# Converting float64 weights with three Vector steps, an intermediate word in PSUM, and banks lent for it

## The chip, the cores and the metric

The kernel runs on one core of a Trainium2 chip. The core has five engines that matter here, each with its own in-order queue: PE (matmuls, with PEld for the loading of its weights), DVE (the Vector engine), ACT (the Scalar engine), POOL (GpSimd) and SP, which issues the DMAs. PSUM, where matmuls write, has eight banks of 2 KiB per partition. The metric is the device time of one execution in microseconds.

## The reference

Inputs are q, k, v of shape 8 x 8 heads x 576 x 64 in float32, and the weights U (576 x 32), V (32 x 576), w_ch1 (512 x 2048) and w_ch2 (2048 x 512). The weights come in as float64.

```python
# attention: pooled by 4 over the sequence, plus local with |i - j| < 4
out_up = np.repeat(sm_attn(q_d, k_d, v_d), 4, axis=2)
scores = np.where(mask, scale * q @ k.T, -1e9)
x = (out_up + softmax(scores) @ v)         # to B, S, 512
# mixing over the sequence and a channel FFN
h = xt @ U @ V
u = x + h.transpose(0, 2, 1)
ch = np.maximum(u @ w_ch1, 0.0) @ w_ch2
return (u + ch).astype(np.float32)
```

## The kernel before

**Precision.** PE multiplies in a reduced float32 form, so u, the hidden layer and the weights are each kept as a high word (H) and a low word (L = value - H). Each product is three matmuls: H by H, H by L, L by H.

**The weights.** `convert` turns float64 words into a float32 value t, then into H and L. A float64 is read as two int32 words, w(1) the high one (sign, 11 bits of exponent, 20 of mantissa), w(0) the low one. For a block of 128 x 512: ACT takes the absolute value of the high word as a float (L341); DVE clamps it (L342), shifts it left by 5 and right by 2 (L344), puts the sign and the top exponent bit back (L347) and puts in the top three bits of the low word (L349); ACT writes H (L351); POOL writes L = t - H (L354). All four DVE steps read and write SBUF. W1 is 16 such blocks (`load_w1`), W2 16 (`load_w2`); U is converted in two layouts (`load_ublk`, early; `load_u`, late) and V in two halves (`load_v`). The raw words of W1, W2 and the late U share three buffers (tag "Pt", with the products of the late attention), taken in the order W1, W2, U.

**The work.** There are 32 pairs of heads (4 for each of 8 batch elements). The first five are "early": their local attention runs on PE (`local_blocks`: scores in `ps_b`, transposes in `ps_bt`, values in `ps_ba`), their pooled attention in `early_global`. The other 27 are "late": pooled attention on PE, the local part as products on POOL (L799) and sums on DVE (L804). `early_mix` and `mix_part` apply U and V and write uH and uL. The FFN then runs over 256 steps (8 batch elements x 2 halves of 288 columns x 16 blocks of the hidden layer). `ffn1` of a step is 12 matmuls into one bank `ps_h` (L888), then ACT writes hH (L895) and DVE hL (L896) from that bank; `ffn2` is 12 matmuls (L911) into four output banks acc0 to acc3, which are kept over 16 steps. `ffn2` of a step is planned three steps after its `ffn1` (LAG = 3) and just ahead of the `ffn1` that is then due. hH has four buffers, hL three.

**PSUM before.** Four banks of one tag each in `ps_acc` (acc0 to acc3): FFN-2's sums, and before them the early scores, alternating between acc0/acc1 and acc2/acc3. Two banks of one tag in `ps_h`: FFN-1, and before it the early transposes and values. Two banks in `ps_m` for everything else.

**What sets the order.** The program lists operations with an engine, an estimated duration, a priority and what they read and write. A planner (`Plan.run`) simulates the five engines with these estimates and writes out each engine's queue; a buffer is granted to the operation that heads its queue (by priority among kinds that share a slot), and freed when its last user is done. On the chip every engine works through its queue in that order. FFN matmuls have the lowest priority and fill what attention leaves. W2 lies in the SBUF of the early attention: "late" is the point at which all early operations are done, and the high words of W2 and FFN-1 steps from 3 on wait for it.

## Time and profile before

| what | value |
|---|---|
| runs of the kernel | 1036.84, 1036.84 and 1039.56 us (median 1036.84) |
| span of the profiled execution, the only time that the page gives of it | 1036.6 us |
| ACT writing H of W1, 16 blocks | 10.0 us, 628 ns each |
| ACT writing H of W2, 16 blocks | 10.0 us, 627 ns each |
| POOL writing L of W1, 16 blocks | 22.8 us, 1425 ns each |
| POOL writing L of W2, 16 blocks | 24.1 us, 1506 ns each |
| loads of W1 and of W2 | 16 DMAs of 512 KB each |

A line of a group names the source line, the engine, the operation, the tile written and the tiles read, the shapes, how often it ran; then the busy time in us and the mean of one in ns; then the idle time of its engine before it and what ended it. A line of windows gives, for a stretch of time, each engine's busy time with the number of its instructions, the granted clock of PE as a share of full speed, the busy share of the DMA engines and GB/s. The chain of waits follows the work that ended last back in time and gives each line's share of the stretch. A line of waits gives the time in total, the number and the longest. A line of the timeline gives the start, the duration, the engine and the operation. "c" is the converted block's tile t of W1 or W2; w1r and w2r are the raw words.

### The profile page before, as it was taken

Reading aid. Unit: us, or ns where it says so; the run is one execution under the profiler, and the core shown is the slowest. Engines: PE = TensorE matmul, PEld = TensorE weight load, DVE = VectorE, ACT = ScalarE, POOL = GpSimd, SP = SyncE. Lnnn points to the kernel's source line nnn. Section 1 sums busy time; section 2 is a strip of 40 time slices with the busy share of each in tenths; the row PEclk is TensorE's granted clock in tenths of the full one; section 3 lists DMA queues with packets and bytes.
Section 4 is the critical chain, followed back from the end, with each engine's and each line's share of the span. In section 5 each row is a group of like instructions: output and inputs, shape, how many; then the busy total and the mean of one; then the engine's idle time right before and its main releaser. Section 6 shows DMA issues by size and latency. Waiting matters only on the chain.

```text
span 1036.6 us, 26946 instructions
## 1 busy us (share of the span) xinstructions
PE 996.9 (96%) x10831; PEld 975.3 (94%) x10831; DVE 529.8 (51%) x1054; ACT 388.0 (37%) x1234; POOL 557.2 (54%) x567
## 2 busy tenths in 40 slices
PE   6778898999999999999999999999999999999998
PEld 5667888999999999999999999999999999999998
DVE  5997898655554545444475344534652544211111
ACT  3676554442443434443344244423443232111110
POOL 4854568788575656565585638762765625211010
PEclk9896999999999999999999999999999999999999
DMA  8866764753555545545555355624644242000000
GB/s 279 226 172 179 199 186 116 149 138 104 135 137 115 141 113 132 128 86 146 120 137 125 87 132 133 143 75 101 151 116 117 64 113 50 24 1 24 1 24 23
DMA packets 222612, 120.30 MB, mean 116 GB/s; under 512 B 175492, under 2 KB 198456, under 8 KB 222488
## 3 DMA queue, kind: packets, MB, share of 16 engines
q1 hardware_dynamic: 222488, 118.58, 45.5%
q8 instruction: 85, 1.39, 0.6%
q14 instruction: 39, 0.32, 0.1%
HBM read 87.78 MB, written 30.75 MB: 114 GB/s over the span
## 4 chain that ended last, share of the span: by engine, by line
PE 84%; DVE 7%; POOL 3%; issue 2%; DMA 2%; ACT 2%; SPq 0%; DVEq 0%; POOLq 0%; ACTq 0%
PE acc L911 36%; PE ps_h L888 35%; PE ps_a L552 2%; PE ps_b L719 2%; DVE c L347 2%; PE ps_hu L848 1%; DVE c L349 1%; PE ps_t L539 1%; DMA w2r<-in_W 1%; PE ps_b L726 1%; POOL Pt L799 1%; DVE c L342 1%; DVE c L344 1%; PE ps_a L484 1%; PE ps_v L431 1%
## 5 line engine op out<-in xcount | busy, mean ns | idle before, releaser
L911 PE MATMUL acc<-hH,W2H 128*128 128x288 f32 x1024 | 310.5, 303 | 0.0
L896 DVE SCALAR_TENSOR_TENSOR hL<-ps_h,hH 128x288 fp32r<-128x288 f32 x256 | 116.6, 455 | 378.6 <-ACT hH L895 378.0
L888 PE MATMUL ps_h<-uH,W1H 128*128 128x288 f32 x1024 | 304.3, 297 | 4.1 <-DVE hL L896 3.1
L911 PE MATMUL acc<-hH,W2L 128*128 128x288 f32 x1024 | 303.1, 296 | 2.6 <-POOL W2L L354 2.6
L888 PE MATMUL ps_h<-uL,W1H 128*128 128x288 f32 x1024 | 303.4, 296 | 1.2 <-POOL uL L871 1.2
L911 PE MATMUL acc<-hL,W2H 128*128 128x288 f32 x1024 | 302.6, 296 | 0.0
L888 PE MATMUL ps_h<-uH,W1L 128*128 128x288 f32 x1024 | 302.0, 295 | 0.0
L799 POOL TENSOR_TENSOR Pt<-vl,at 128x896 f32<-128x896 f32 (+1 forms) x135 | 233.4, 1809 | 115.1 <-DVE acc L804 61.1
L895 ACT ACTIVATE hH<-ps_h 128x288 fp32r<-128x288 f32 x256 | 105.1, 410 | 433.6 <-PE ps_h L888 433.5
L888 PEld LDWEIGHTS ps_h<-uH,W1H 128*128 128x128 f32 x1024 | 193.5, 189 | 5.4 <-DVE hL L896 3.8
L911 PEld LDWEIGHTS acc<-hH,W2L 128*128 128x128 f32 x1024 | 193.2, 189 | 3.5 <-POOL W2L L354 3.5
L888 PEld LDWEIGHTS ps_h<-uL,W1H 128*128 128x128 f32 x1024 | 193.4, 189 | 1.5 <-POOL uL L871 1.5
L911 PEld LDWEIGHTS acc<-hH,W2H 128*128 128x128 f32 x1024 | 193.3, 189 | 1.1
L888 PEld LDWEIGHTS ps_h<-uH,W1L 128*128 128x128 f32 x1024 | 193.7, 189 | 0.0
L911 PEld LDWEIGHTS acc<-hL,W2H 128*128 128x128 f32 x1024 | 193.7, 189 | 0.0
L804 DVE TENSOR_REDUCE acc<-Pt 128x128 f32<-128x1024 f32 (+1 forms) x135 | 144.7, 1103 | 4.7 <-POOL Pt L799 2.3
L871 POOL TENSOR_TENSOR uL<-xT,uH 128x288 fp32r<-128x288 f32 x56 | 44.1, 811 | 71.3 <-ACT uH L869 71.2
L921 POOL TENSOR_TENSOR o<-uH,uL 128x288 f32<-128x288 f32 x64 | 49.8, 816 | 54.2 <-DMA out_t<-o 54.2
L840 POOL TENSOR_TENSOR xL<-xL,xH 116x640 fp32r<-116x640 f32 x28 | 44.0, 1572 | 64.2 <-ACT xH L839 49.3
L510 POOL TENSOR_TENSOR vr<-vr 72x256 f32<-72x256 f32 x54 | 42.4, 785 | 46.9 <-DMA vr<-in_v 46.8
L793 ACT ACTIVATE Pt<-ul 128x128 f32<-128x128 f32 (+1 forms) x135 | 48.4, 441 | 21.3 <-DVE acc L804 20.0
L744 ACT ACTIVATE se<-ps_b 96x114 f32<-96x114 f32 x108 | 38.5, 357 | 47.1 <-PE ps_b L719 34.1
(129 smaller groups left out, 1106.9 us busy)
## 6 DMA issues: line engine op xcount, KB each, us to landing
vl<-in_vp SPq DMA_DIRECT2D x54, 240.0 KB
out_t<-o SPq DMA_DIRECT2D x64, 144.0 KB
w1r<-in_W SPq DMA_DIRECT2D x16, 512.0 KB
w2r<-in_W SPq DMA_DIRECT2D x16, 512.0 KB
Y<-x_s SPq DMA_DIRECT2D x112, 72.0 KB
gT<-in_kT SPq DMA_DIRECT2D x27, 291.0 KB
xL<-x_s SPq DMA_DIRECT2D x28, 280.0 KB
gq<-in_qT SPq DMA_DIRECT2D x27, 288.0 KB
```

What stands on the lines that cost most here:

```text
L510: pool_tt(256, lambda x=x: nc.gpsimd.tensor_tensor(out=x()[:, :, 0:2, :], in0=x()[:, :, 0:2, :], in1=x()[:, :, 2:4, :], op=ALU.add), [x], ...
L744: act(n * KL, lambda p=ps[hh], se=se, n=n, rows=rows: nc.scalar.activation(se()[rows, 0:n].rearrange("p r k -> p (r k)"), p()[rows, 0:n * ...
L793: act(n * D, lambda n=n, ps=ps, Pt=Pt: nc.scalar.activation(Pt()[:, :n, :, 7], ul()[:, ps, :], AF.Copy), [ul], [(Pt, 1)], prio, 0.16)
L799: nc.gpsimd.tensor_tensor(out=Pt()[:, :n, :, 0:7].rearrange("p s d o -> p o s d"), in0=win, in1=at()[:, ps, :].rearrange("p s o -> p o s") ...
L804: dve(8.5 * n * D, lambda n=n, ps=ps, Pt=Pt: nc.vector.tensor_reduce(out=acc()[:, ps, :], in_=Pt()[:, :n], axis=AX.X, op=ALU.add), [(Pt, 0 ...
L840: pool_tt(640, lambda: nc.gpsimd.tensor_tensor(out=xL(), in0=xL().bitcast(F32), in1=xH().bitcast(F32), op=ALU.subtract), [xL, xH], [xL], prio)
L871: pool_tt(TN, lambda uH=uH, uL=uL, uf=uf: nc.gpsimd.tensor_tensor(out=uL()[:, hp, :], in0=uf(), in1=uH()[:, hp, :].bitcast(F32), op=ALU.su ...
L888: nc.tensor.matmul(ps()[:, :TN], w[:, dc, fs], u()[:, dc, :], start=(n == 0), stop=(n == 3 * NDC - 1))
L895: last_h[i] = act(TN, lambda: nc.scalar.activation(hH(), ps()[:, :TN], AF.Relu), [ps], [hH], FIRST, 0.05)
L896: dve(TN, lambda: nc.vector.scalar_tensor_tensor(hL(), ps()[:, :TN], 0.0, hH().bitcast(F32), op0=ALU.max, op1=ALU.subtract), [ps, hH], [hL ...
L911: nc.tensor.matmul(ac[e]()[:, :TN], W2[w][:, fc, es], hx(), start=(fc == 0 and n == 0), stop=(fc == NFC - 1 and n == 2))
L921: pool_tt(TN, lambda e=e, o1=o1: nc.gpsimd.tensor_tensor(out=o1()[:, :TN], in0=uH()[:, e, :].bitcast(F32), in1=uL()[:, e, :].bitcast(F32), ...
```

## The change

`convert` loses the clamp. ACT now copies the high word with a scale of 2^-112, which moves the exponent's bias; DVE shifts that left by 3 into a tile y in PSUM, puts the sign from w(1) into y, and then writes t from y and w(0). y lies in the second FFN-1 bank (h1) for W2 and for the late U, and else in acc2 and acc3 by turns. The early scores use acc0 and acc1 alone. The two `ps_h` banks have a tag each: FFN-1 steps 0 to 18 use h0 only, later ones h0 and h1 by turns, and from step 19 on each FFN-1 also depends on the one before it in the plan. The first FFN-2 step waits for the high words of all W1 blocks. The estimated durations of the conversion's DVE steps are new as well.

```diff
@@ -16,8 +16,6 @@
 AF = mybir.ActivationFunctionType
 ALU = mybir.AluOpType
 AX = mybir.AxisListType
-F_MIN = float(np.uint32(0x38000000).view(np.float32))
-F_MAX = float(np.uint32(0x47EFE000).view(np.float32))
 
 PE, DVE, ACT, POOL, SP = range(5)
 SLACK_FROM = 80
@@ -223,6 +221,7 @@
     PWx = 0.5
     pw = lambda prio: PW0 if prio < 10 else PWx
     W1P = 20
+    H1 = NFC + LAG
     NE = 5
     CN = 512
     QL, KL = 32, 38
@@ -243,7 +242,7 @@
     ffn = ctx.enter_context(tc.tile_pool(name="ffn", bufs=1))
     dram = ctx.enter_context(tc.tile_pool(name="dram", bufs=1, space=bass.MemoryType.DRAM))
     ps_acc = ctx.enter_context(tc.tile_pool(name="ps_acc", bufs=1, space=bass.MemoryType.PSUM))
-    ps_h = ctx.enter_context(tc.tile_pool(name="ps_h", bufs=2, space=bass.MemoryType.PSUM))
+    ps_h = ctx.enter_context(tc.tile_pool(name="ps_h", bufs=1, space=bass.MemoryType.PSUM))
     ps_m = ctx.enter_context(tc.tile_pool(name="ps_m", bufs=2, space=bass.MemoryType.PSUM))
 
     def psum(pool, name, tag, bufs):
@@ -295,6 +294,7 @@
     pat_sb = early_pool.tile([128, KW - KL], F32, name="pat_sb")
     Ublk = early_pool.tile([128, NS, 2 * R], F32, name="Ublk")
     kept = {}
+    count = {"y": 0}
 
     def ring(shape, name, n=2):
         if name not in kept:
@@ -334,20 +334,23 @@
 
     def convert(raw, pp, n, hi_out, lo_out, a, wkey, name, prio, gate=(), l0=0):
         t = buf(ffn, [128, CN], I32, name, "cT:" + name, 3)
+        if gate or name == "cu" and lo_out is not None:
+            y = buf(ps_h, [128, CN], I32, "y_h", "h1:" + name, 1)
+        else:
+            count["y"] += 1
+            y = buf(ps_acc, [128, CN], I32, "y_a", f"acc{2 + count['y'] % 2}:{name}", 1)
         w = lambda i: raw()[:pp, :2 * n].rearrange("p (n two) -> p n two", two=2)[:, :, i]
         ti = lambda: t()[:pp, :n]
-        tf = lambda: t()[:pp, :n].bitcast(F32)
-        ta = lambda: tf().rearrange("p (a n) -> p a n", a=a)
-        act(n, lambda: nc.scalar.activation(tf(), w(1).bitcast(F32), AF.Abs), [raw], [t], prio)
-        dve(1.6 * n, lambda: nc.vector.tensor_scalar(
-            out=tf(), in0=tf(), scalar1=F_MIN, scalar2=F_MAX, op0=ALU.max, op1=ALU.min), [t], [t], prio, True)
-        dve(1.6 * n, lambda: nc.vector.tensor_scalar(
-            out=ti(), in0=ti(), scalar1=5, scalar2=2, op0=ALU.logical_shift_left,
-            op1=ALU.logical_shift_right), [t], [t], prio, True)
-        dve(1.2 * n, lambda: nc.vector.scalar_tensor_tensor(
-            ti(), w(1), -0x40000000, ti(), op0=ALU.bitwise_and, op1=ALU.bitwise_or), [raw, t], [t], prio)
-        dve(1.2 * n, lambda: nc.vector.scalar_tensor_tensor(
-            ti(), w(0), 29, ti(), op0=ALU.logical_shift_right, op1=ALU.bitwise_or), [raw, t], [t], prio)
+        yi = lambda: y()[:pp, :n]
+        ta = lambda: ti().bitcast(F32).rearrange("p (a n) -> p a n", a=a)
+        act(n, lambda: nc.scalar.activation(
+            ti().bitcast(F32), w(1).bitcast(F32), AF.Copy, scale=2.0 ** -112), [raw], [t], prio)
+        dve(n, lambda: nc.vector.tensor_scalar(
+            out=yi(), in0=ti(), scalar1=3, scalar2=None, op0=ALU.logical_shift_left), [t], [y], prio)
+        dve(1.15 * n, lambda: nc.vector.scalar_tensor_tensor(
+            yi(), w(1), -0x80000000, yi(), op0=ALU.bitwise_and, op1=ALU.bitwise_or), [raw, y], [y], prio)
+        dve(1.15 * n, lambda: nc.vector.scalar_tensor_tensor(
+            ti(), w(0), 29, yi(), op0=ALU.logical_shift_right, op1=ALU.bitwise_or), [raw, y], [t], prio)
         act(n, lambda: nc.scalar.activation(hi_out(), ta(), AF.Copy), [t, *gate], [wkey + "H"], prio)
         if lo_out is None:
             return
@@ -407,7 +410,6 @@
 
     heads = [slice(hh * D, (hh + 1) * D) for hh in range(2)]
     CROSS = ((0, 0), (1, 0), (2, 0), (2, 1), (3, 1), (4, 1))
-    count = {"b": 0}
 
     def pool_halves(raw, lo, out, e, prio):
         gh = work(e, glo, [128, SD, 2], F32, "gh")
@@ -604,8 +606,7 @@
     def local_blocks(b, hp, x_s, qt, kt, vw_t, prio):
         ob = buf(early_pool, [128, NS, 2, D], F32, "ob", None, 2)
         view = lambda t: t()[:, :NS * KL].rearrange("p (r k) -> p r k", r=NS)
-        ps = [psum(ps_acc, "ps_b", f"acc{2 * (count['b'] % 2) + hh}", 1) for hh in range(2)]
-        count["b"] += 1
+        ps = [psum(ps_acc, "ps_b", f"acc{hh}", 1) for hh in range(2)]
 
         def s_mm():
             for hh in range(2):
@@ -635,7 +636,7 @@
             mk + [ri], mk, prio, 1.9)
         et = buf(early_pool, [128, NS, 128], F32, "et", None, 2)
         for r0, r1 in ((0, 3), (3, NS)):
-            pt = psum(ps_h, "ps_bt", "h:e", 2)
+            pt = psum(ps_h, "ps_bt", f"h{r0 > 0:d}:e", 1)
             cols = lambda t, m=r1 - r0: t()[:, :m * 128].rearrange("p (r q) -> p r q", r=m)
 
             def t_mm(pt=pt, r0=r0, r1=r1, cols=cols):
@@ -644,7 +645,7 @@
             op(PE, pw(prio) * 0.24 * (r1 - r0), t_mm, mk + [(ms, "pat"), "ident"], [pt], prio)
             act((r1 - r0) * 128, lambda pt=pt, r0=r0, r1=r1, cols=cols: nc.scalar.activation(
                 et()[:, r0:r1], cols(pt), AF.Copy), [pt], [(et, r0)], prio, 0.05)
-        pa = psum_pair(ps_h, "ps_ba", "h:e", 2)
+        pa = [psum(ps_h, "ps_ba", f"h{hh}:e", 1) for hh in range(2)]
         av = lambda t: t()[:, :NS * D].rearrange("p (r d) -> p r d", r=NS)
 
         def a_mm():
@@ -872,13 +873,13 @@
                 out=uL()[:, hp, :], in0=uf(), in1=uH()[:, hp, :].bitcast(F32), op=ALU.subtract),
                 [ufk, (uH, hp)], [(uL, hp)], prio)
 
-    hbuf, accs, last_h = {}, {}, {}
+    hbuf, accs, last_h, mm_op = {}, {}, {}, {}
     FIRST, FILL = -10.0, 1000.0
 
     def ffn1(s, i):
         b, t, fc = s
         uH, uL = u_of(b, t)
-        ps = psum(ps_h, "ps_h", "h", 2)
+        ps = psum(ps_h, "ps_h", f"h{i % 2 * (i >= H1):d}:f", 1)
         fs = slice(fc * 128, (fc + 1) * 128)
 
         def mm():
@@ -889,7 +890,8 @@
                                      start=(n == 0), stop=(n == 3 * NDC - 1))
                     n += 1
         ur = [(uH, c) for c in range(NDC)] + [(uL, c) for c in range(NDC)]
-        op(PE, PH, mm, ur + [f"W1_{fc}H", f"W1_{fc}L"] + ["late"] * (i >= 3), [ps], FILL + i)
+        mm_op[i] = op(PE, PH, mm, ur + [f"W1_{fc}H", f"W1_{fc}L"] + ["late"] * (i >= 3), [ps], FILL + i,
+                      [mm_op[i - 1]] if i >= H1 else ())
         hH = buf(ffn, [128, TN], F32R, "hH", bufs=4)
         hL = buf(ffn, [128, TN], F32R, "hL", bufs=3)
         last_h[i] = act(TN, lambda: nc.scalar.activation(hH(), ps()[:, :TN], AF.Relu), [ps], [hH], FIRST, 0.05)
@@ -910,7 +912,8 @@
                 for n, (w, hx) in enumerate((("H", hH), ("H", hL), ("L", hH))):
                     nc.tensor.matmul(ac[e]()[:, :TN], W2[w][:, fc, es], hx(),
                                      start=(fc == 0 and n == 0), stop=(fc == NFC - 1 and n == 2))
-            op(PE, PF, mm, [hH, hL, f"W2_{fc}H", f"W2_{fc}L"], [ac[e]], FILL + i + LAG - 0.5)
+            first = [f"W1_{f}H" for f in range(NFC)] * (i == 0)
+            op(PE, PF, mm, [hH, hL, f"W2_{fc}H", f"W2_{fc}L"] + first, [ac[e]], FILL + i + LAG - 0.5)
         if fc == NFC - 1:
             uH, uL = u_of(b, t)
             for e in range(NDC):
```

## The prediction

> **What bounds the kernel now.** I read the page's head first, then the windows of the span, then the chain of waits, and last the groups by line inside the stretch that the windows single out.
>
> ```profile
> span 1036.6 us, 26946 instructions
> PE 996.9 (96%) x10831; PEld 975.3 (94%) x10831; DVE 529.8 (51%) x1054; ACT 388.0 (37%) x1234; POOL 557.2 (54%) x567
> ...
> core 0: us, PE busy (x) PEld busy (x) DVE busy (x) ACT busy (x) POOL busy (x), PEclk, DMA share, GB/s
> ...
> 10.00:100.00 90.00, 73.15 (x1200) 62.06 (x1201) 73.93 (x151) 56.60 (x176) 52.01 (x53) 0.85 0.74 214
> 100.00:166.00 66.00, 59.58 (x691) 56.28 (x690) 60.14 (x101) 35.15 (x94) 41.36 (x35) 0.95 0.67 183
> 166.00:1000.00 834.00, 829.52 (x8620) 823.03 (x8621) 384.48 (x780) 290.41 (x953) 460.43 (x468) 1.00 0.43 103
> 1000.00:1037.00 37.00, 33.06 (x250) 32.83 (x248) 6.26 (x14) 3.84 (x10) 0.00 (x0) 0.98 0.05 17
> ```
>
> From 166 us to 1000 us PE is busy 829.52 of 834 us at full clock: nothing done to DVE there can shorten it. Before that PE has gaps and a lower clock, and DVE is the fullest engine (73.93 of 90 us, then 60.14 of 66). So the change is worth what it brings forward before 166 us. A ceiling: PE's busy time scaled to full clock is 73.15 x 0.85 = 62 of 90 us and 59.58 x 0.95 = 57 of 66 us, so about 28 us can be won between 10 and 100 us and 9 us between 100 and 166 us, 37 in all. The first is generous, because "busy" counts pipelined matmuls whole and the first head pair has to be loaded.
>
> The chain of waits between 10 and 166 us, then between 100 and 166 us, and who holds up the DMA issues:
>
> ```profile
> by line: DVE c L347 11.5%; issue 7.8%; DVE c L349 7.5%; DMA w2r<-in_W 6.4%; DVE c L342 5.8%; DVE c L344 5.7%; PE ps_a L484 5.1%; PE ps_v L431 4.7%; DMA Y<-x_s 3.7%; DMA pool_sb<-in_pool 3.4%; PE ps_hu L677 3.2%; ACT E_e L459 2.7%; POOL W2L
> by line: DVE c L347 13.1%; issue 11.3%; DVE c L342 8.9%; DMA Y<-x_s 8.7%; DVE c L344 8.6%; DMA w2r<-in_W 7.2%; POOL W2L L354 6.3%; PE acc L911 5.8%; DVE c L349 5.5%; DVE hL L896 3.5%; PE ps_h L888 2.9%; DVE cu L347 2.6%; SPq L833 2.2%; ACT
> ...
> SPq L389 <- DVE c L349: 22.3, 10, 4.2
> ```
>
> The four DVE lines of the conversion hold 11.5 + 7.5 + 5.8 + 5.7 = 30.5% of 156 us, 47.6 us; of that 36.1% of 66 us, 23.8 us, lie in the second stretch and 23.8 us in the first. SP, whose queue also carries the attention's loads and stores, stood 22.3 us before W1 loads whose buffer the last conversion step still read.
>
> **Part 1: the conversion's DVE work.** Before, by shape:
>
> ```profile
> L342 DVE TENSOR_SCALAR c<-c 128x512 f32<-128x512 f32 x32 | 19.2, 602 | 7.0 <-ACT c L341 6.9
> L347 DVE SCALAR_TENSOR_TENSOR c<-w2r,c 128x512 int32<-128x512 int32 x16 | 17.5, 1094 | 0.2
> L347 DVE SCALAR_TENSOR_TENSOR c<-w1r,c 128x512 int32<-128x512 int32 x16 | 17.1, 1066 | 0.4
> L344 DVE TENSOR_SCALAR c<-c 128x512 int32<-128x512 int32 x32 | 16.9, 529 | 0.4
> L349 DVE SCALAR_TENSOR_TENSOR c<-w1r,c 128x512 int32<-128x512 int32 x16 | 15.3, 953 | 0.2
> L349 DVE SCALAR_TENSOR_TENSOR c<-w2r,c 128x512 int32<-128x512 int32 x16 | 14.2, 886 | 0.1
> ...
> 137.97 0.41 DVE L342 TENSOR_SCALAR c<-c 128x512 f32<-128x512 f32 x1
> ...
> 156.90 4.02 DVE L342 TENSOR_SCALAR c<-c 128x512 f32<-128x512 f32 x1
> ...
> 161.82 0.68 DVE L347 SCALAR_TENSOR_TENSOR c<-w2r,c 128x512 int32<-128x512 int32 x1
> ...
> 157.54 1.98 POOL L799 TENSOR_TENSOR Pt<-vl,at 128x896 f32<-128x896 f32 x1
> 159.35 1.28 POOL L354 TENSOR_TENSOR W2L<-c,W2H 128x512 fp32r<-128x512 f32 x1
> ...
> L700 DVE TENSOR_TENSOR uL<-ps_u,uH 128x288 fp32r<-128x288 f32 x8 | 3.4, 449 | 0.9 <-ACT uH L698 0.9
> ...
> L924 DVE TENSOR_TENSOR o<-acc,o 128x288 f32<-128x288 f32 x64 | 26.6, 453 | 21.0 <-PE acc L911 20.4 <-issue 0.2
> L770 DVE SCALAR_TENSOR_TENSOR ms<-sc,mask_sb 128x63 f32<-128x63 f32 x27 | 12.9, 478 | 0.0
> ```
>
> The six groups are 100.2 us for 32 blocks, 3.13 us a block. The same operation takes 0.41 or 4.02 us (L342), and 0.68 us undisturbed against a mean of 1.09 (L347). The 4.02 us one lay under POOL's product (L799) and low-word subtraction (L354) and ended 0.3 us after them, at 160.9 against 160.6. Stretched like that are the forms that take two SBUF inputs or run at the faster rate from SBUF to SBUF: L770, with two SBUF inputs and 63 elements, means 478 ns. L700 and L924, with one input in PSUM and one in SBUF, keep 449 and 453 ns early and over the whole run, though POOL is over half busy. The change puts the intermediate word in PSUM, so that each of the three new DVE steps has at most one SBUF operand on either side: they belong to the second kind.
>
> The clamp (L342) goes. The shift loses the fast rate: between 0.41 us and 0.68 us, the undisturbed full-rate price of 512 elements; I take 0.68, since no row with a PSUM operand ran faster. The two others I put at 0.68 each. New: 3 x 0.68 = 2.04 us a block, 65 us for 32, 35 us of DVE less. The four small conversions (V in two halves, U in two layouts) go the same way; they are few, and I count nothing for them on the path. ACT keeps two operations of the same sizes (the scaled copy in place of the absolute value); POOL keeps one. No DMA is added, and SP's order moves only with the buffers.
>
> [...] The next row is a PSUM form beside L770.
>
> ```profile
> L487 DVE TENSOR_TENSOR od<-ps_a,ri 72x128 f32<-72x128 f32 x10 | 2.8, 276 | 3.7 <-PE ps_a L484 3.6
> ...
> L770 DVE SCALAR_TENSOR_TENSOR ms<-sc,mask_sb 128x63 f32<-128x63 f32 x3 | 0.6, 211 | 0.0
> ```
>
> From 63 elements at 211 ns (L770 while undisturbed, before 166 us) to 512 at 680 ns is 1.04 ns an element; 128 elements would take 279 ns, and the PSUM form took 276. No surcharge for PSUM shows. [...]
>
> **What of it lies on the path.** The conversion's share of the chain falls by 1 - 2.04/3.13 = 35%: 8.3 us in each stretch. In the first stretch SP also stands less before W1 loads; a third of 22.3 us less waiting is 7 us, of which I count 3 because other loads lie ready behind only some of them: 11 us. What is late next there is the early attention's own ladder (ps_v, ps_a, exponentials) and PE at 0.85 clock. In the second stretch only 9 us of PE time is free, and PE becomes late next as soon as W2 arrives faster: I count 5 us of the 8.3. Together 16.
>
> **Part 2: the banks lent.** Early score blocks use two output banks instead of alternating four; their DVE readers free a pair long before the next pair of heads is loaded, so nothing. The first FFN-2 step waits for all W1 high words:
>
> ```profile
> 94.05 0.64 ACT L351 ACTIVATE W1H<-c 128x512 fp32r<-128x512 f32 x1 [1.39 <-DVE c L349]
> ...
> 103.27 0.58 PE L911 MATMUL acc<-hH,W2H 128*128 128x288 f32 x1
> ```
>
> The last was there 8.6 us before the first FFN-2 matmul: nothing, and at most the time by which W2 block 0 overtakes, some 2 us. Converting W2 in the second FFN-1 bank shares it with the early transposes; a shift that waits there holds all DVE work behind it, but those uses end as W2 begins: nothing to 2 us.
>
> The real price is the single FFN-1 bank for steps 0 to 18. FFN-1 step i+1 now waits for hL of step i, and behind it on PE stand FFN-2 and attention matmuls, and behind these ACT and DVE. The best and the worst case of such a loop:
>
> ```profile
> 967.62 0.29 PE L888 MATMUL ps_h<-uH,W1L 128*128 128x288 f32 x1
> 967.95 0.41 ACT L895 ACTIVATE hH<-ps_h 128x288 fp32r<-128x288 f32 x1 [2.76 <-PE ps_h L888]
> 968.39 0.46 DVE L896 SCALAR_TENSOR_TENSOR hL<-ps_h,hH 128x288 fp32r<-128x288 f32 x1 [2.71 <-ACT hH L895]
> 969.35 0.30 PE L888 MATMUL ps_h<-uH,W1H 128*128 128x288 f32 x1
> ...
> 111.45 0.40 PE L888 MATMUL ps_h<-uH,W1H 128*128 128x288 f32 x1 [1.37 <-DVE hL L896]
> ```
>
> With FFN-2 between, hL ends at 968.85 and the next FFN-1 starts at 969.35: 0.5 us to spare if ACT and DVE are free. Without cover it costs 1.37 us. Over the 16 steps from 3 to 18 that is 0 to 22 us. Early on ACT and DVE are not always free, but a conversion step ahead in DVE's queue is only 0.68 us; I take 0.2 us a step, 3 us, nearer to the row with cover, because FFN-2 goes ahead of FFN-1 in the plan.
>
> The planner's costs for the conversion change too, and with them the order of every queue. After 166 us PE has only 4.5 us of gaps to lose or fill (834 - 829.5) before the tail, so I take nothing for that.
>
> **The sum**: 1036.6 - 16 + 3 = 1023.6 us of span. The median of the runs stands 0.2 us above the profiled span: **1023.8 us**.
>
> **Rivals.**
> 1. The early ladder loosens more than its share of the chain, because SP, ACT and DVE are in-order queues and each late conversion held others: up to the ceiling, 28 us and more, about 1009 us. For it speak SP's 22.3 us; against it that DMA is busy 0.74 already and ps_a, ps_v stay.
> 2. Another resource is late at once (loads of W1 and W2, 0.74 and 0.67 of the DMA engines before): the 47.6 us of chain only change their name. About 4 us won, 1033 us.
> 3. PSUM does not free DVE from POOL. Then each step costs the mean of the old two-input ones, 64.1 us / 64 = 1.0, 3.0 a block against 3.13: 2 us won, 3 lost, 1037.6 us. L700 and L924 speak against it.
> 4. Slower: the single bank. If every one of 16 loops is uncovered, 22 us are lost against 16 won: 1043 us. It decides from 1.0 us a step on. For it speaks that DVE is over 80% busy there; against it the cover of an FFN-2 group, 1.7 us from 967.62 to 969.35, and a DVE that the change itself unloads.
>
> **How the numbers follow.** My forecast (1013 to 1031 us) 61%, rival 1 12%, rival 2 11%, rival 3 4%, rival 4 12%. About 0.3%, 3.1 us, is what a measurement can tell from no change. Faster: 61 + 12 + 6 of rival 2 = 79%; the same: 5 of rival 2, all of rival 3 and 1 of rival 4 = 10%; slower: 11%. The range 1005 to 1035 us leaves out rivals 3 and 4 and the low end of rival 1, some 19%.
>
> **What would show it.** Right: the three new DVE steps at 0.6 to 0.7 us each with little spread; POOL's low-word subtractions (L354) shorter as well; PE full from about 150 us instead of 166; the first FFN-2 matmul near 92 us instead of 103. Wrong: new steps with means near 1 us; PE waits on hL (L896) between FFN-1 steps of over 0.5 us each before all W2 is converted; the ladder's own PE and ACT lines taking the chain's share with the first FFN-2 still near 100 us; or PE idle after 166 us, which I hold unchanged.

## The result, and the profile after

The changed kernel takes 1031.97 us (median of 6 runs, 1029.96 to 1036.07) against 1036.97 us for the kernel before beside it. The ratio is 0.9944 with a 95% interval of [0.9924, 0.9964]: 5 us are won where 13 were forecast. The profiled execution took 1032.15 us, 1.85 above its span.

The head of the page of the changed kernel, and its windows (columns as in the forecast):

```profile
span 1030.3 us, 26938 instructions
PE 995.5 (97%) x10831; PEld 975.6 (95%) x10831; DVE 488.6 (47%) x1018; ACT 387.3 (38%) x1234; POOL 539.1 (52%) x567
...
10.00:100.00 90.00, 72.09 (x1289) 60.96 (x1287) 61.10 (x137) 56.49 (x176) 42.16 (x53) 0.81 0.74 226
100.00:166.00 66.00, 60.61 (x619) 58.62 (x611) 43.49 (x92) 38.91 (x112) 43.39 (x44) 0.92 0.68 170
166.00:1000.00 834.00, 834.00 (x8659) 827.94 (x8658) 373.70 (x769) 286.79 (x936) 450.15 (x459) 1.00 0.43 103
```

DVE lost its work: 73.93 to 61.10 us in the first stretch, 60.14 to 43.49 in the second. PE did not follow. In the first stretch it still stands 90 - 72.09 = 17.9 us (16.9 before), and its granted clock fell from 0.85 to 0.81. In the second it stands 5.4 us (6.4 before) at 0.92 (0.95 before). From 166 to 1000 us it is full, where it stood 4.48 us before. 2.0 us of that, and a half clock behind it (0.50 to 0.52 from 169 to 172 us), lay just after 166 us in the kernel before:

```profile
166.00:180.00 14.00, 11.98 (x88) 11.97 (x89) 11.79 (x27) 6.87 (x26) 12.51 (x16) 0.88 0.36 104
...
168.02 0.52 PE L848 MATMUL ps_hu<-xH,Ust 116*64 116x128 f32 x5 [2.50 <-POOL Ust L354]
```

PE waited there for the low word of the late U, which POOL wrote from 167.45 us, behind a conversion that had stood in DVE's queue among the last blocks of W2. The run "before, small W1 loads" below, with the same queues, repeats the wait (2.5 us) and the 0.88. In the changed kernel POOL writes that word from 157.19 us and PE doesn't wait. The other waits of that row were 1.2 us for POOL's uL at 232 us, 0.8 for hL at 235 and 0.5 for `stk` at 754.

The conversion by shape, 10 to 166 us of the changed kernel:

```profile
L357 POOL TENSOR_TENSOR W2L<-c,W2H 128x512 fp32r<-128x512 f32 x16 | 20.7, 1296 | 19.9 <-ACT W2H L354 19.9
L357 POOL TENSOR_TENSOR W1L<-c,W1H 128x512 fp32r<-128x512 f32 x16 | 20.6, 1289 | 31.8 <-ACT W1H L354 30.8 <-ACT nb L456 1.0
...
L348 DVE TENSOR_SCALAR y_h<-c 128x512 int32<-128x512 int32 x16 | 11.0, 690 | 12.9 <-ACT c L346 10.4 <-ACT ob L660 2.2
L350 DVE SCALAR_TENSOR_TENSOR y_a<-w1r,y_a 128x512 int32<-128x512 int32 x16 | 11.0, 690 | 0.3
L350 DVE SCALAR_TENSOR_TENSOR y_h<-w2r,y_h 128x512 int32<-128x512 int32 x16 | 11.0, 689 | 0.2
L352 DVE SCALAR_TENSOR_TENSOR c<-w2r,y_h 128x512 int32<-128x512 int32 x16 | 10.9, 680 | 0.6
L352 DVE SCALAR_TENSOR_TENSOR c<-w1r,y_a 128x512 int32<-128x512 int32 x16 | 10.9, 679 | 0.3
L348 DVE TENSOR_SCALAR y_a<-c 128x512 int32<-128x512 int32 x16 | 10.9, 684 | 1.7 <-ACT c L346 1.6
```

All six groups lie at 679 to 690 ns: 2.06 us a block, and POOL's subtraction fell from 1425 and 1506 to 1289 and 1296 ns. The engine does what was forecast of it. What comes after is the question. The chain of waits of the changed kernel, first for 10 to 100 us, then for 100 to 166, and two rows of SP's waits (10 to 166 us):

```profile
by line: PE ps_v L433 12.3%; PE ps_a L486 7.3%; DMA vw<-up_e 6.6%; DMA sc<-s_s 6.0%; PE ps_hu L678 5.2%; issue 5.2%; DVE y_a L350 4.5%; DVE y_a L348 4.1%; PE ps_bt L644 4.0%; ACT E_e L461 3.8%; PE ps_u L695 3.2%; DMA s_s<-se 3.2%; PE ps_ba 
by line: DMA w2r<-in_W 28.9%; PE ps_h L889 10.7%; PE acc L913 8.6%; DMA xL<-x_s 6.8%; SPq L563 6.4%; DMA ur<-in_U 6.0%; issue 4.1%; ACT c L346 3.5%; ACT E L527 2.7%; ACT se L745 2.3%; DVE hL L898 2.1%; DVE y_h L348 1.9%; ACT hH L897 1.7%; P
...
SPq L493 <- DVE od L489: 16.0, 7, 10.2
SPq L392 <- DVE c L352: 13.9, 8, 3.2
```

The conversion's share changed its name. In the first stretch the early attention's own lines (ps_v, ps_a, vw, sc, E_e) hold the chain, in the second the loads of W2. SP's wait for the conversion before W1 loads fell from 22.3 to 13.9 us, and it now stands 16.0 us, once 10.2, before the store of `od`, with the next W1 and W2 loads behind it. Before, that store's waits were spread over several names (4.1 us on `od`, 5.1 on `c` L344 and smaller ones). All waits of each source line together, from 10 to 100 us, went from 23.4 to 17.3 us for the W1 loads, from 13.8 to 16.9 for the store, and from 58.6 to 56.2 for SP in all.

Two marks of the first stretch are used from here on: the last early ps_ba, which releases "late", and the first FFN-2 matmul (acc). The changed kernel's, and PE's three long waits in that stretch:

```profile
65.93 1.70 PE L678 MATMUL ps_hu<-ob,Ublk 128*64 128x128 f32 x10 [2.80 <-DVE y_a L348]
90.75 1.42 PE L541 MATMUL ps_t<-ident_sb,E 72*72 72x72 f32 x8 [2.51 <-ACT E L527]
92.10 1.41 PE L656 MATMUL ps_ba<-vw,et 46*32 46x64 f32 x80
...
98.22 0.47 PE L727 MATMUL ps_b<-smk,smq 64*32 64x144 f32 x6 [2.61 <-POOL smk L419]
...
103.05 0.44 PE L913 MATMUL acc<-hH,W2H 128*128 128x288 f32 x1
```

Before, the last ps_ba was at 89.48 and the first FFN-2 at 103.27. Neither came forward in this profile. How far such marks scatter is seen in the run with eight gaps at the end of the experiments, which has the changed kernel's queues up to its first gap at 399 us: its last ps_ba came at 87.35 and its first FFN-2 at 101.85, with PE at a clock of 0.86 and 23.1 us of standing from 10 to 100 us. It is called the repeat below.

**A measure of PE's work.** PE's busy time is not a count of its work: an FFN matmul is 0.29 us long in the timeline, but in a row the next one starts 0.132 us later (395.79 to 398.96 us of the run with eight gaps), and at half clock 0.24 us later (403.56 to 406.44 us). So for each run I also counted the matmuls of each line that had begun by a given time and took each at its line's spacing at full clock (0.132 us for an FFN matmul). Before, that is 57.5 us by 100 us, 124.6 by 180 and 192.6 by 250; after, 58.4, 129.1 and 199.2. The 6.6 us at 250 agree with the 6.3 us between the spans. About 1 us of them had been won by 100 us. By 166 us, where the forecast's second stretch ends, the two are still level within 1 us: 396 FFN matmuls had begun before, 387 after, and 20 short ones of the attention more after. The repeat, with 402, is 2 us ahead. So most of the gain was made behind 166 us.

### The profile page after: what moved, and what is told of

Read it like the earlier page. It is cut to its first block, busy times and chain, and to the rows that moved or that the text cites. A ratio compares the mean times of both kernels' runs of the same rounds, so it can differ in the third digit from the quotient of the medians.

```text
span 1030.3 us, 26938 instructions
## 1 busy us (share of the span) xinstructions
PE 995.5 (97%) x10831; PEld 975.6 (95%) x10831; DVE 488.6 (47%) x1018; ACT 387.3 (38%) x1234; POOL 539.1 (52%) x567
## 4 chain that ended last, share of the span: by engine, by line
PE 89%; DMA 5%; ACT 2%; DVE 2%; issue 1%; SPq 1%; DVEq 0%; ACTq 0%
PE acc L913 38%; PE ps_h L889 38%; PE ps_a L554 2%; PE ps_b L720 2%; DMA w2r<-in_W 2%; PE ps_hu L849 2%; PE ps_t L541 1%; PE ps_v L433 1%; PE ps_b L727 1%; PE ps_u L864 1%; PE ps_a L486 1%; DMA vw<-up_e 1%; DMA sc<-s_s 1%; DMA pool_sb<-in_pool 0%; PE ps_hu L678 0%
## 5 line engine op out<-in xcount | busy, mean ns | idle before, releaser
L512 POOL TENSOR_TENSOR vr<-vr 72x256 f32<-72x256 f32 x54 | 39.8, 738 | 30.5 <-DMA vr<-in_v 30.1
```

The costliest lines, as they stand in the source:

```text
L512: pool_tt(256, lambda x=x: nc.gpsimd.tensor_tensor(out=x()[:, :, 0:2, :], in0=x()[:, :, 0:2, :], in1=x()[:, :, 2:4, :], op=ALU.add), [x], ...
```

## The experiments

All ratios are to the kernel before, run beside it on the same chip; times from different chips aren't compared directly. The ratio to beat, or to explain, is 0.9944. Code is shown in extracts; "..." marks what is left out.

### Is it PSUM, or the step that was dropped?

**Three steps, all in SBUF** (the kernel before with the new arithmetic):

```diff
-        act(n, lambda: nc.scalar.activation(tf(), w(1).bitcast(F32), AF.Abs), [raw], [t], prio)
+        act(n, lambda: nc.scalar.activation(
+            ti().bitcast(F32), w(1).bitcast(F32), AF.Copy, scale=2.0 ** -112), [raw], [t], prio)
...
-            out=tf(), in0=tf(), scalar1=F_MIN, scalar2=F_MAX, op0=ALU.max, op1=ALU.min), [t], [t], prio, True)
-        dve(1.6 * n, lambda: nc.vector.tensor_scalar(
-            out=ti(), in0=ti(), scalar1=5, scalar2=2, op0=ALU.logical_shift_left,
-            op1=ALU.logical_shift_right), [t], [t], prio, True)
+            out=ti(), in0=ti(), scalar1=3, scalar2=None, op0=ALU.logical_shift_left), [t], [t], prio, True)
```

> The kernel before with the three-step conversion, whose intermediate word stays in SBUF, and the banks as before. Three theories of why only about 5 of the 13 us came. Loads: once DVE is lighter, the weight loads (DMA time and SP's in-order queue) come late, so a cheaper conversion wins the same few us however it is made; here the steps are still held up by POOL (I expect a mean near 2.5 us a block against 3.13 and 2.05), and the time is 1031 to 1035 us. Banks: the single FFN-1 bank gives back some 6 us or more; here, with both banks, the time is 1026 to 1029 us though DVE works longer. Vector: DVE's time still sets the pace; then the time lies by DVE's time between the two kernels, near 1034 us.

Measured: 1.0008 [0.999, 1.0025]. The steps took 628 ns (shift) and 811 to 1072 ns (the two others), 81.3 us in all against 100.2. A step less, and no time won. The plan made another order of it, with the first FFN-2 at 108.56 us.

**The changed kernel, queues unchanged, with y in SBUF:**

```diff
-        yi = lambda: y()[:pp, :n]
+        yi = ti
```

> The changed kernel instruction for instruction in the same order and with the same waits, but the intermediate word lies in SBUF, in the converted tile. If PSUM is what frees DVE from POOL: the three steps mean 0.62, 1.0 and 0.95 us with a wide spread, some 18 us more of DVE time, and by the rate of the other runs (10.6 us for 65 us of DVE) 3 us slower than the changed kernel; if the order of the queues is what made the gain: within 2 us of the changed kernel.

Measured: 0.9999 [0.998, 1.0017]. Its groups by shape, 10 to 166 us:

```profile
L348 DVE TENSOR_SCALAR c<-c 128x512 int32<-128x512 int32 x32 | 18.2, 572 | 9.5 <-ACT c L346 9.1
L352 DVE SCALAR_TENSOR_TENSOR c<-w2r,c 128x512 int32<-128x512 int32 x16 | 17.3, 1082 | 0.2
L350 DVE SCALAR_TENSOR_TENSOR c<-w2r,c 128x512 int32<-128x512 int32 x16 | 15.1, 942 | 0.2
L352 DVE SCALAR_TENSOR_TENSOR c<-w1r,c 128x512 int32<-128x512 int32 x16 | 13.9, 871 | 0.1
L350 DVE SCALAR_TENSOR_TENSOR c<-w1r,c 128x512 int32<-128x512 int32 x16 | 13.8, 862 | 0.3
```

The two-input steps cost 862 to 1082 ns with two SBUF inputs and 679 to 690 with one. With the same queues the place of the intermediate word is the whole gain of the change. The 78.3 us of this run's DVE steps against 65.7 make 12.6 us of DVE, and some 6 us of time. The first FFN-2 is at 108.12 us here: with these queues PSUM brought it forward by 5 us, to 103.05. But the kernel before, with slower steps and its own queues, had it at 103.27.

### Does the single FFN-1 bank cost anything?

**The banks alone** (the kernel before with the changed kernel's PSUM tags, old conversion):

```diff
...
-        ps = psum(ps_h, "ps_h", "h", 2)
+        ps = psum(ps_h, "ps_h", f"h{i % 2 * (i >= H1):d}:f", 1)
...
```

> The changed kernel's bank layout and waits with the old four-step conversion in SBUF. Banks theory: 5 us or more slower than before, 1042 us and above, with PE waiting on hL (before FFN-1) for 6 us or more before 166 us. Loads and Vector theories: within 3 us of before, 1035 to 1040 us.

Measured: 1.0018 [0.9998, 1.0037]. PE waited more for hL (10 to 200 us; the first row is this run, the second the kernel before), but the time rose by at most 0.4%, 3.8 us. The last ps_ba came at 97.28 and the first FFN-2 at 107.75, 7.8 and 4.5 us later than before; which of the banks or of the order that the plan makes with them did that, no run separates:

```profile
PE ps_h L888 <- DVE hL L897: 8.2, 7, 2.2
```

```profile
PE ps_h L888 <- DVE hL L896: 2.3, 2, 1.4
```

**Later W2 loads in the plan.** In the changed kernel (10 to 166 us) PE waited for hL, as ACT and DVE stood before W2 loads that landed later than planned (ACT 10.0 us for the loads, DVE 10.4 us for ACT's copies of them; the three loads on the chain landed 5.51 to 7.89 us after issue):

```profile
PE ps_h L889 <- DVE hL L898: 5.9, 4, 2.3
```

```diff
-            [], [raw], prio, 525)
+            [], [raw], prio, 525, lat=4.3)
```

> The changed kernel with the planner told that a W2 load lands 3 us later (its loads took 5.4 to 7.9 us from issue where the planner reckons 3.4), so that ACT's and DVE's queues hold other work ahead of the conversion. If late W2 loads at the head of ACT's and DVE's queues are what holds hL and so FFN-1 between 100 and 166 us: PE's waits on hL there fall from 5.9 us to under 3 us, and the time by 2 to 5 us. If the single bank holds FFN-1 by itself: no change in those waits.

Measured: 0.9932 [0.9906, 0.9958]. PE's waits on hL are gone, the time is that of the changed kernel. In this order the last ps_ba came at 86.85 and the first FFN-2 at 96.85, and still no time was won: PE stood 9.2 us from 100 to 166 (5.4 in the changed kernel) and 1.9 behind it. **Other estimates for the DVE steps** (n to 1.15 n, 1.15 n to 1.3 n):

> The changed kernel with the planner's durations of the three DVE steps raised to 1.15, 1.3 and 1.3 of n (0.68 to 0.76 us each against 0.60 to 0.68), and nothing else: how far the time moves by another order alone. If the order is a matter of chance at this size: up to 5 us either way. If not: within 1.5 us.

Measured: 0.9926 [0.99, 0.9951]. These two orders differ from the changed kernel's by 1 to 2 us, within the intervals. No price of the single bank is seen, but one of up to 3.8 us isn't excluded by the run with the banks alone.

### What is late in the first stretch?

**No DVE steps at all** (all three left out):

> The changed kernel without the three DVE steps of the conversion (ACT's scaled copy goes straight on to H and L), so that the weights are wrong; some 68 us of DVE work are left out. Vector theory: 10 us or more below the changed kernel. Loads theory: at most 4 us below it, 1028 to 1032 us, with weight loads at the head of the chain of waits. Banks theory: also near it, with PE's waits on hL unchanged.

Measured: 0.9838 [0.981, 0.9865]. Some 11 us are won over the changed kernel, but work by 100 us is 58.4, as with the steps (the order is another one here too). **One W1 block in place of 16** (loads and conversions of 15 left out):

> The changed kernel with 15 of the 16 blocks of W1 left out (loads and conversions), every FFN-1 step taking its weights from block 0; the result is wrong by that. The run without DVE steps did no more PE work by 100 us than the kernels with them (58.4 us of it against 57.5 before). Ladder theory (the early attention's chain of PE, ACT and DVE steps, at a PE clock of 0.7 to 0.9, sets the first 100 us, whatever the weights cost): PE work by 100 us stays within 3 us of 58 plus FFN, the early pairs end no more than 5 us sooner, and the time is 1015 to 1028 us. Loads theory (W1's 8 MB and SP's queue set it): the last early pair ends 10 us or more sooner and the time is below 1012 us.

Measured: 0.9788 [0.9761, 0.9814]; work by 100 us 66.6, last ps_ba at 82.1. So the W1 pipeline holds back the first stretch by some 8 us of work, and DVE's part alone doesn't account for that.

**Half of the loads** (every second block takes the raw words of its neighbour):

> The changed kernel, but every second block of W1 and W2 is converted from the raw words of the block ahead of it, so that half of the weight loads (8 of 16 MB and 16 of 32 DMAs) are left out and the raw buffers reach twice as far ahead; the weights are then wrong by that. Loads theory: 6 us or more below the changed kernel, 1026 us or less. Banks theory: within 3 us of the changed kernel, since FFN-1 still waits for its one bank. Vector theory: within 2 us of it.

Measured: 1.0208. It says nothing on loads: a raw buffer is now held over two blocks, the plan moved, and PE was busy only 32.22 of the 66 us from 100 to 166.

The next four keep every queue as it is and shrink one resource. The first replaces each W1 load by an eighth that the conversion reads eight times, the second lets the three DVE steps of W1 and W2 treat 16 columns, the third does both, the fourth is the first in the kernel before.

```diff
-            out=raw(), in_=w1.bitcast(I32)[f],
+            out=raw()[:, 0:128], in_=w1.bitcast(I32)[f][:, 0:128],
...
-            out=yi(), in0=ti(), scalar1=3, scalar2=None, op0=ALU.logical_shift_left), [t], [y], prio)
+            out=sh(yi()), in0=sh(ti()), scalar1=3, scalar2=None, op0=ALU.logical_shift_left), [t], [y], prio)
```

> The changed kernel with the same plan and order, in which each W1 load carries an eighth of its block (64 KB) and the conversion reads that eighth eight times over, so ScalarE's, VectorE's and GpSimd's instructions keep their number and size. If the W1 transfers took the path when VectorE left it, PE's work done by 100 us rises from 58.4 to 64 us or more (66.6 with the loads and conversions both left out), the last early ps_ba comes near 82 to 86 us and the time falls about 8 us below the changed kernel, ratio 0.985. If ScalarE's and GpSimd's conversion work or the ladder's own steps hold it, work by 100 us stays at 57 to 60 and the ratio at 0.991 to 0.996.

> The changed kernel with the same plan and order, in which the three VectorE steps of each W1 and W2 block treat 16 columns instead of 512, so VectorE loses some 55 us of work and nothing else changes. If VectorE has left the path of the first stretch, PE's work by 100 us stays at 57 to 60 and only the second stretch gains, 8 to 10 us as with the steps left out (ratio 0.984). If VectorE is still late in the first stretch, work by 100 us rises to 62 or more and the ratio falls below 0.980.

> Both edits together: small W1 loads and short VectorE steps, same plan and order. If transfers and VectorE each hide behind the other, the two together win more in the first stretch than their sum: work by 100 us of 66 or more. If the ladder's own steps at the low granted clock are the floor of the first stretch, work by 100 us stays near 60 here too.

> The kernel before, same plan and order, with each W1 load carrying an eighth. If VectorE held the first stretch there, as the forecast had it, small loads win nothing by 100 us (57.5 to 59) and the ratio is 0.995 to 1.000. If the transfers already held it beside VectorE, work by 100 us rises to 61 or more and the ratio falls to 0.990 or less.

| kernel | ratio, 95% | last ps_ba | first FFN-2 | work by 100 us | PE standing, clock, 10 to 100 us |
|---|---|---|---|---|---|
| before | 1 | 89.48 | 103.27 | 57.5 | 16.9, 0.85 |
| changed | 0.9944 [0.9924, 0.9964] | 92.10 | 103.05 | 58.4 | 17.9, 0.81 |
| small W1 loads | 0.9936 [0.991, 0.9963] | 87.20 | 99.46 | 60.6 | 20.6, 0.87 |
| short DVE steps | 0.9899 [0.9857, 0.994] | 89.28 | 101.39 | 59.3 | 19.1, 0.83 |
| both | 0.9875 [0.984, 0.991] | 83.23 | 95.03 | 64.8 | 18.4, 0.89 |
| before, small W1 loads | 0.9993 [0.997, 1.0016] | 90.76 | 102.61 | 58.2 | 20.0, 0.85 |
| changed, the repeat | (gaps from 399 us on) | 87.35 | 101.85 | 58.9 | 23.1, 0.86 |

Taking the transfers away wins 2.2 us of work by 100 us, DVE's steps 0.9, both 6.4; in the kernel before the transfers win 0.7. These are single profiles, and the times' intervals overlap, so the sizes are rough. The last row is the control: with nothing shrunk, the repeat lies 4.8 us earlier at the last ps_ba than the changed kernel's profile, and 0.5 us (4 FFN matmuls) ahead in work. So what DVE's steps win by themselves is hardly more than this scatter, and so are the marks with small loads, though not their 2.2 us of work. Only the run with both stands clear of it throughout. That speaks for transfers and DVE standing side by side, each late when the other is taken away. With both gone PE still stands 18.4 us.

**The collision in SP's queue.** In the changed kernel the raw buffers come free earlier, three W1 loads go out at 63 us, and the 36 KB load vw<-up_e, issued at 62.53 ahead of them but behind another W1 load of 60.62, one of 144 KB and two of 216 KB, holds the chain for 5.92 us. Here the ladder's small transfers are issued from ACT's queue:

```diff
...
-            dma(lambda hh=hh: nc.sync.dma_start(
+            dma_act(lambda hh=hh: nc.scalar.dma_start(
...
```

> The changed kernel, with the early ladder's small transfers (stores up_e of od, loads vw of up_e) issued from ScalarE's queue instead of SP's; the large W1 and W2 loads stay on SP's. In the changed kernel vw<-up_e, issued at 62.53, landed only near 68.5 us behind W1 loads, and SP then stood 10.2 us before od with the next W1 and W2 loads behind it. If that collision in SP's queue is what ate the first stretch's gain, the last early ps_ba moves from 92.1 to 86 us or earlier, SP's wait on od goes from 16.0 us in all to under 4, and the time falls by 3 to 6 us to a ratio of about 0.990 of the kernel before. If the ladder's own PE and ACT steps at a low granted clock are what is late, the last ps_ba stays at 90 to 93 us and the ratio at 0.993 to 0.996. If a load in another queue still lands late because the 16 DMA engines are full, vw<-up_e still takes over 4 us from issue to landing in 60 to 70 us.

Measured: 0.9921 [0.9903, 0.9939]. SP's waits, 40 to 100 us:

```profile
SPq L581 <- PE ps_ba L660: 13.4, 3, 9.2
SPq L396 <- DVE c L356: 12.6, 7, 2.9
```

The wait on `od` is gone, one of 9.2 us for ps_ba has come, and the last ps_ba is at 91.46, not 86. The queue is not what the gain was lost in; 2 us may be won, which the intervals don't separate from none. **With the later W2 loads as well:**

> The small transfers on ScalarE's queue, and W2 loads told to land 3 us later. If the two losses (the small transfers in the first stretch, 3 to 6 us, and PE's 5.9 us of waits on hL behind late W2 loads in the second) are both real and add up, the ratio is about 0.985 to 0.988; if the second costs nothing, as the later W2 landing alone showed, it is that of the run with the small transfers on ScalarE's queue alone within 0.003.

Measured: 0.9959 [0.9944, 0.9975]. The two don't add up: 0.985 to 0.988 would have been their sum, and the ratio lies even above that of the small transfers alone. **A slower DMA rate in the plan** (200 KB/us in place of 290 for early work):

> The changed kernel, with the planner told that transfers of early priorities move 200 KB/us instead of 290, so that it spaces the W1 loads wider. If the collision of W1 loads with the ladder's small loads holds the first stretch, it is the wider order that helps: DMA share below 0.9 in 60 to 70 us, last early ps_ba before 90 us, ratio 0.990. If order alone is worth little, as with the other estimates for VectorE, the ratio stays at 0.992 to 0.997.

Measured: 1.0131 [1.0108, 1.0153]. The planner also spread the ladder's own transfers: the last ps_ba came at 103.04, the last high word of W1 was there at 108.91 (88.75 in the changed kernel), and the first FFN-2 came at 119.09 us. Which of the two sets the end of this stretch the run doesn't tell; an order that delays both by 11 to 20 us costs 19 us of time.

### The half clock

Between the changed kernel and the three shrunk ones PE is about as long busy from 60 to 80 us. What differs is its clock (changed, small loads, short steps, both, and last the repeat with nothing shrunk; the column before the last two):

```profile
60.00:80.00 20.00, 16.11 (x245) 13.70 (x243) 12.41 (x26) 14.02 (x40) 6.63 (x6) 0.74 0.53 156
```

```profile
60.00:80.00 20.00, 15.70 (x227) 13.67 (x210) 15.49 (x32) 15.22 (x44) 9.21 (x8) 0.91 0.31 80
```

```profile
60.00:80.00 20.00, 15.29 (x212) 13.38 (x195) 5.60 (x27) 14.40 (x43) 8.44 (x8) 0.83 0.57 170
```

```profile
60.00:80.00 20.00, 16.13 (x289) 14.52 (x289) 6.92 (x32) 15.95 (x45) 8.40 (x7) 1.00 0.37 99
```

```profile
60.00:80.00 20.00, 15.47 (x218) 13.53 (x203) 15.39 (x32) 15.24 (x44) 9.17 (x8) 0.91 0.67 193
```

The repeat has 0.91 as well. The lower clock of the changed kernel's profile in this window is thus not bound to its loads or DVE steps.

Finer windows of the changed kernel show where the 0.74 comes from:

```profile
64.00:68.00 4.00, 2.04 (x12) 1.48 (x12) 3.80 (x7) 3.65 (x16) 2.54 (x3) 0.84 1.00 209
68.00:72.00 4.00, 3.41 (x90) 3.27 (x91) 0.28 (x1) 1.27 (x3) 2.00 (x2) 0.50 0.80 290
72.00:76.00 4.00, 3.87 (x18) 3.35 (x18) 1.68 (x4) 3.30 (x8) 0.00 (x0) 0.50 0.00 0
76.00:80.00 4.00, 3.67 (x29) 3.19 (x27) 2.68 (x7) 2.03 (x5) 0.00 (x0) 0.88 0.04 9
```

PE stands 2.8 us to 65.9, the clock falls to 0.50 and stays there until 76, though PE is busy again. Behind the same wait the repeat was back at 1.00 by 68 us (0.57 from 64 to 68, 1.00 from 68 to 72). The same follows the waits that end at 90.8 and 98.2: 0.50 from 91 to 104. Two runs put 20 transposes of the identity on PE's queue ahead of each of the three waiting groups; the second of them adds 8 ahead of two early ps_a:

```diff
...
         def hu():
+            fill(ph, "hu", {2: 20})
...
```

> The changed kernel, plan and order kept, with 20 transposes of the identity (nobody reads them) put on PE's queue ahead of three groups before which PE stood 2.5 to 2.8 us in the changed kernel: the third early mix (ps_hu, 65.9 us), the first late attention's transposes (ps_t, 90.8) and the second late pair's scores (ps_b, 98.2). After the waits the granted clock there went to 0.50 from 67 to 76 and from 91 to 104 us. If what the first stretch lost is this half clock after a gap, the clock stays near 1.00 from 67 to 76 and from 91 to 104, the last early ps_ba moves from 92.1 to 88 us or earlier, and 4 to 10 us are won: ratio 0.985 to 0.991. If the clock is only a companion and the ladder is held by its ScalarE and DMA steps, the ratio stays at 0.993 to 0.997, and it rises to 0.998 if the 5 us of transposes come in the way.

> The same, with 8 more such transposes ahead of the third and the fifth early ps_a (26.3 and 37.0 us), after whose waits of 1.2 to 1.4 us the clock was 0.50 from 26 to 32 and from 36 to 42. By the half-clock theory another 2 to 5 us by 50 us: the first ps_ba before 42 us instead of 44.1 and the ratio 0.003 below that of the three fills. If those two drops come from the low activity before 24 us and not from these waits, the two runs agree within 0.002.

Measured: 0.9955 [0.9932, 0.9978] and 0.9946 [0.9928, 0.9964], with the last ps_ba at 95.0 and 94.9. They don't decide it. The first two of these fills waited for the PSUM bank of their group, so they ran behind the gap (the run with three fills):

```profile
66.28 4.07 PE L262 MATMUL ps_hu<-ident_sb 128*128 128x128 f32 x20 [3.23 <-DVE y_a L355]
...
90.64 3.93 PE L262 MATMUL ps_t<-ident_sb 128*128 128x128 f32 x20 [2.52 <-ACT E L535]
```

With PE kept full the clock was back at 1.00 by 70 and 94 us, in place of 76 and 104. Only the second of these says something for the fill, since the repeat without it has 68 and 102. The 4 us of each fill may have taken what that won. The last run measures the gap by itself, where PE never stands:

```diff
...
         def mm():
+            if i in range(80, 240, 20):
+                nc.tensor.transpose(ps()[:, :128], ident_sb, ident_sb)
+                nc.scalar.activation(idle, ps()[:, :128], AF.Copy)
+                for _ in range(9):
+                    nc.scalar.activation(idle, idle, AF.Copy)
+                nc.tensor.transpose(ps()[:, :128], idle, ident_sb)
...
```

> The changed kernel with PE made to stand still eight times in the stretch where it otherwise never does: ahead of FFN-1 steps 80, 100 and so on to 220 a transpose, ten copies of 128x128 in a row on ScalarE and a second transpose that waits for the last copy, some 3 us each (10 x 0.25 us and the hand-overs). If a standstill of PE costs itself alone, the time rises by 8 x 3 = 24 us, at most 30. If the granted clock falls to 0.50 after each, as behind the gaps of 2 to 3 us in the first stretch (67 to 76 and 91 to 104 us), each adds half of some 4 to 9 us at half clock: 16 to 36 us more, 40 to 66 in all. PE's granted clock in the 6 us behind each gap tells which.

Measured: 1.0368 [1.0341, 1.0395], so 1.0368 - 0.9944 = 4.2%, 44 us, over the changed kernel. One gap of this run in the timeline, the windows around the first, and the 12 us behind the first two gaps:

```profile
484.29 0.47 PE L892 MATMUL ps_h<-ident_sb,idle 128*128 128x128 f32 x1 [3.44 <-ACT idle L891]
```

```profile
401.00:402.00 1.00, 0.00 (x0) 0.00 (x0) 0.00 (x0) 0.91 (x4) 0.92 (x2) 1.00 1.04 248
402.00:403.00 1.00, 0.20 (x2) 0.20 (x2) 0.07 (x1) 0.83 (x4) 0.05 (x1) 0.55 0.88 273
403.00:404.00 1.00, 1.00 (x5) 1.00 (x5) 0.59 (x3) 0.21 (x1) 0.02 (x1) 0.50 0.55 159
404.00:408.00 4.00, 4.00 (x18) 4.00 (x18) 0.46 (x1) 0.41 (x1) 4.00 (x3) 0.50 0.00 1
408.00:409.00 1.00, 1.00 (x6) 1.00 (x5) 0.00 (x0) 0.00 (x0) 1.00 (x1) 0.54 0.00 0
409.00:410.00 1.00, 1.00 (x10) 1.00 (x9) 0.00 (x0) 0.00 (x0) 0.85 (x2) 1.00 0.00 0
```

```profile
401.80:413.80 12.00, 11.00 (x146) 10.81 (x152) 3.24 (x9) 2.06 (x7) 6.59 (x6) 0.72 0.15 42
483.29:495.29 12.00, 11.00 (x84) 11.00 (x85) 2.62 (x5) 2.75 (x8) 4.62 (x8) 0.86 0.33 89
```

The eight gaps are 27.5 us. Behind three of them the 12 us ran at a mean clock of 0.72, behind five at 0.86: 12 x (3 x 0.28 + 5 x 0.14) = 18.5 us lost. Together 46 us, against 44 measured. So a standstill of 3.4 us costs 5 to 7 us: itself, and 1.7 or 3.4 us through the half clock behind it. By the mean clocks the half clock lasts 0.14 x 12 / 0.5 = 3.4 us or twice that here, and up to 13 us in the first stretch (91 to 104), where PE has further short waits. Standstills shorter than these of 3.4 us had a half clock behind them as well: 2.50 us at 168 us of the kernel before, and the 2.80 us above.

## Why the prediction was wrong

**What bounds the kernel** was right in its outline and wrong in one premise. Of the row from 166 to 1000 us the prediction says that nothing done to DVE there can shorten it, and takes nothing for its 4.5 us of gaps. They all closed. With the half clock of 14 x 0.12 = 1.7 us from 166 to 180, that is 6.2 us, as much as the 6.3 us between the two spans. 3.7 of them are the end of DVE's own backlog: DVE was busy all 16 us from 150 to 166 before, the late U was converted last, and PE stood for it (2.0 us of that wait behind 166) and then ran at half clock. The prediction counted nothing on the path for the four small conversions, of which this is one. Why the other waits (2.5 us, most of them at 232 to 235 us) went is not tested. The ceiling for the first stretch was no ceiling of what DVE can give either. It counted PE's standing time and its half clock as time that the conversion could free. PE stands 16.9 us there before, 17.9 after (23.1 in the repeat), 18.4 with neither full W1 loads nor DVE steps.

**Part 1** was right in size and cause. Forecast 2.04 us a block at 0.68 us a step, measured 2.06 at 0.68 to 0.69; the steps are uniform, and POOL's subtraction became shorter. PSUM does free DVE from POOL (rival 3 falls): with y in SBUF the two-input steps take 862 to 1082 ns and the whole gain goes. A surcharge for a PSUM operand does not show: the two-input steps with one took 679 to 690 ns, L347 with two SBUF inputs 0.68 us undisturbed.

**What of it lies on the path** is the step that failed: 11 us in the first stretch and 5 in the second, 16 by 166 us. Measured is about 1 us of PE work by 100 us, and by 166 us the two kernels are level within 1 us, or 2 us apart by the repeat. The step took the conversion's share of the chain of waits (23.8 us in each stretch) times the share of it that DVE saves, as if a share of the chain were time that is won when its line gets faster.

What stood in its place in the first stretch is shown in part. The W1 transfers run beside DVE's steps: without both, work by 100 us rose by 6.4 us, without DVE's steps alone by 0.9, hardly more than the 0.5 by which two profiles of the same queues differ. Even with no DVE steps in the conversion, work by 100 us was that of the changed kernel. The 3 us put down for SP's shorter waits weren't won either: by source line SP stood 6.1 us less before W1 loads and 3.1 us more before the store of `od`, 2.4 us less in all. What isn't separated is the order of the queues, for which the prediction took nothing. The three newly planned kernels with the conversion all in SBUF (fewer steps, lent banks, and both) had their first FFN-2 at 107.75 to 108.56 us, against 103.27 before. These are single profiles, but so the new order, with the banks, may have put the ladder (the early attention's chain) back by about the 5 us that PSUM then brought it forward. No run has the queues of the kernel before with the intermediate word in PSUM, so this stays open.

The granted clock is not shown to be part of that failure. The step named "PE at 0.85 clock" as late next, but as a constant. It follows PE's gaps and scatters: 0.81 in the changed kernel's profile, 0.86 in the repeat, so its fall is no price of the change. What a gap costs through the clock is shown where PE is the bound. Whether the half clock holds back the ladder stays open: in the repeat it was shorter and the ladder ended 4.8 us sooner, but one pair of profiles doesn't tell cause from effect, and the fills didn't get into the gaps.

**The second term**, 5 us in the second stretch, met the size of the whole gain by luck. "PE becomes late next as soon as W2 arrives faster" came about only from about 150 us on. W2's loads hold 28.9% of the chain from 100 to 166, and PE waited 5.9 us on hL behind them.

**Part 2**, 3 us for the single FFN-1 bank, is neither shown nor excluded. The banks alone gave 1.0018 [0.9998, 1.0037], 0 to 3.8 us, and taking the waits on hL away in the changed kernel gave no time. Rival 4 (22 us) falls.

So 0 to 2 us by 166 us, with whatever the bank costs inside, and some 5 us behind it stand where 11 + 5 - 3 and nothing were forecast. **Rival 2** came nearest, with 1033 us against 1031.97: another resource late at once, the chain changing its names. By the work done that held up to 166 us. Where the time was won, it did not name. Of the signs named, PE full from about 150 us did come: 29.9 busy of the 30 us from 150 to 180, against 25.5 before. The first FFN-2 near 92 us did not, and the sign of error given for that, the ladder's own lines on the chain with the first FFN-2 still near 100, is what the profile shows. No run here is clearly faster than the changed kernel with the whole work done; the small transfers on ACT's queue come nearest (0.9921), within the intervals.

## What to carry to other kernels

A line's share of the chain of waits says where the chain ran, not what is won when the line gets faster: ask which other queue is nearly as late in the same stretch, and shrink both in a test with the queues unchanged. Repeat a profile before reading a mark of it: the same queues put one mark 4.8 us apart. Look too at the short gaps behind the stretch that is to get faster; here the end of the busy engine's backlog lay in them, and with it much of the gain. Where PE is the bound, count a gap of 3.4 us as 5 to 7, as the eight gaps here cost, and look for what closes the gap first. Where a step has two SBUF inputs beside a busy POOL, try an intermediate word in PSUM: here it took the step from 862 to 1082 ns to 679 to 690; whether that wins time depends on what else is late.

## What the runs showed of the hardware

- Each of eight standstills of PE of 3.44 us was followed by 3.4 or 6.8 us at half clock, in a stretch that had run at full clock before. By the windows around the first gap (0.55 in 402 to 403, 0.54 in 408 to 409) the clock fell about 402.1, 2.7 us after PE stopped at 399.4, and rose about 408.9.
- The same two-input DVE step on 512 elements took 862 to 1082 ns with both inputs in SBUF and 679 to 690 ns with one in PSUM, and POOL's subtraction 1289 and 1296 ns in place of 1425 and 1506 once DVE worked in PSUM (1470 and 1466 with the changed kernel's queues and the word in SBUF). The relief goes both ways.
- In the changed kernel a 36 KB load, issued within 2 us of loads of 512, 144 and twice 216 KB ahead of it, held the chain for 5.92 us.
